# Attention scores in 128x64 tiles, small steps moved between engines, and all weight conversions in the attention stage

## The chip, the cores and the metric

One core of a Trainium2 chip. The metric is the device time of one execution in microseconds (us), the median of several runs. TensorE multiplies (PE; its weight loads are PEld), VectorE (DVE), ScalarE (ACT) and GpSimd (POOL) do the rest, SyncE (SP) issues most of the DMA transfers.

## What is computed

Three stages follow each other. q, k and v are (4, 8, 1152, 64): 4 batches, 8 heads. All arithmetic is fp32 in and out.

```python
def _attn_ref(q, k, v):
    q_pool = q.reshape(B, H, S // 2, 2, D).mean(axis=3)
    scores = scale * np.matmul(q_pool, k.transpose(0, 1, 3, 2))
    scores = scores - np.max(scores, axis=-1, keepdims=True)
    attn = np.exp(scores)
    attn = attn / (np.sum(attn, axis=-1, keepdims=True) + 1e-09)
    return np.matmul(attn, v)
...
# x: the attention's output as 2304 tokens of 512
    logits = x @ w_gate + modality_bias[modality_id]      # 8 experts
    e_idx = np.argmax(logits, axis=1)
    ...
        out[mask] = gate_w[mask, None] * (np.maximum(x[mask] @ w1[e], 0.0) @ w2[e])
...
    h = x @ w_in                                          # 512 -> 2048
    g = np.maximum(h, 0.0) + np.log1p(np.exp(-np.abs(h)))
    return g @ w_out                                      # 2048 -> 512
```

## The kernel before

**Attention** works on 16 pairs of heads, `p`. For each pair the 576 pooled queries come in two halves of 288, the 1152 keys in nine chunks of 128; a round `g` is one chunk of one half, so a pair has 18 rounds and the whole 288. In each round TensorE makes the scores of both heads (`smat`, L163: keys as weights, 288 queries streaming, a high and a low fp16 product each, into PSUM tile `st`), ScalarE takes their exponential (`ex`, L170, tile `P`), GpSimd adds `P` up over three chunks (`add`, L174, tile `acc`; a few sums on VectorE where the table `DVA` says so), and TensorE multiplies `P` with the values (`pv`, L207; fp32, 64 columns of weights for each head, written side by side into two halves of one PSUM tile; it runs for two rounds at a time). Ahead of a pair its row maxima have to be known: `srow` (L109) makes 27 row scores per pair (queries as weights, 384 keys streaming, tile `sr`), VectorE reduces each to a maximum (L121); `mfin` (L123) gathers them, splits them into a high and a low part `nh` and has TensorE write them into the second half of `Q` (L140). Row scores have full width, but for one tile in nine whose two halves are two heads (L120).

`casts` (L72) prepares a pair: pooled queries `qs` (L77), fp16 casts of queries and keys (ScalarE), their low parts (L86 queries, L94 keys, GpSimd). `lstage` (L217) is the routing of half a batch: logits, maximum, one-hot of the expert, rank in the expert, gate; some thirty steps on 96 partitions, each put into a round of its own by `LSTEPS`. After the first rounds the order on every engine in this stage is the one in which the code is written: in each round the next scores, an event or two of that round in turn with row scores, `pv`, the sums.

**Conversions.** `w_in` and `w_out` come as 8-byte floats; a conversion (`convert`, L984) loads 512 KB of them and makes 128x512 fp32 numbers in three integer steps on VectorE (L993 to L995). There are 32. `CH` places 12 of them in attention, with a staging tile `stg` of two buffers; the other 20 run in the experts' stage (`CVN`: behind units 2, 6 and 10 of a block), in the four buffers `mraw` that the experts' weights use too.

**The experts' stage** (`Moe`, L625, and `moe_ffn`, L724) has nine blocks of 256 tokens of one expert, 16 units of 12 products each. `split` (L642) makes a high (ScalarE) and a low fp16 half (VectorE, L653; in each eighth one GpSimd, L650 and L651) of the loaded weights. The splits of the dense weights (L741) run here too. Here TensorE and SyncE keep the written order, and a scheduler sets that of the other engines. **The dense stage** (`Ffn`) follows.

Of the kernel before, what the change touches and what calls it, by code (L numbers as in the profile page):

```python
# [16 lines left out]
def attention(ctx,late,tc,I,C,x_dram,LG,gate,fill,early):  # L17

    nc=tc.nc
# [52 lines left out]
    def casts(p):  # L72
        ka,kb,q=KA[p%NS],KB[p%NS],Q[p%NS]; ve=nc.gpsimd if p==1 else nc.vector
# [22 lines left out]
        if p==0:  # L96
            c0(); cq(0,0)(); ck(0,0)(); cl(0)(); ck(0,1)(); cq(1,0)(); ck(1,0)(); ck(1,1)()
            C['cl1']=cl(1)
            for h in range(2):
# [4 lines left out]
                (7,cq(0,1)),(9,cq(1,1)),(6,ckl(0,0)),(7,ckl(0,1)),(9,ckl(1,0)),(11,ckl(1,1))]  # L104
# [4 lines left out]
    def srow(r):  # L109
        p,w=divmod(r,SRN); t,kh=divmod(w,3)  # L110
        ka,q=KA[p%NS],Q[p%NS]
        if w==0: MX[p]=smp.tile([128,9,3],F32,name="mx")
        sr=srp.tile([128,512],F32,name="sr")
        h,r0=TILES[t]
        k0=kh*KW
        if h<2:
            nc.tensor.matmul(sr[:,:KW],lhsT=q[:,h,0,r0:r0+128],rhs=ka[:,h,k0:k0+KW],start=True,stop=True)  # L117
        else:
            for hh in range(2):
                nc.tensor.matmul(sr[64*hh:64*hh+64,:KW],lhsT=q[:,hh,0,r0:r0+64],rhs=ka[:,hh,k0:k0+KW],start=True,stop=True)  # L120
        nc.vector.tensor_reduce(out=MX[p][:,t,kh:kh+1],in_=sr[:,:KW],axis=AX.X,op=ALU.max,negate=True)  # L121

    def mfin(p,ta=0,tb=9):  # L123
# [30 lines left out]
        return [a,b,c(0),c(1)]+([d(0),d(1)] if ta==0 else [])  # L154
# [19 lines left out]
    def add(g):  # L174

        p,half,c=dec(g)
        for n,G in enumerate(groups(p,half)):
# [7 lines left out]
            else:  # L185
                for h in range(2): nc.gpsimd.tensor_tensor(out=A[:,h],in0=B_[:,h],in1=P[g][:,h],op=ALU.add)  # L186
# [30 lines left out]
    def lstage(b,half,last=False):  # L217

# [38 lines left out]
        def eq():  # L257
            V.scalar_tensor_tensor(out=T('eq',[96,3,8]),in0=z['d'],scalar=0.0,in1=C['iotaE8'].unsqueeze(1).to_broadcast([96,3,8]),op0=ALU.is_equal,op1=ALU.mult)
        def ed():
            nc.scalar.activation(out=T('ed',[96,3,8]),in_=z['d'],func=ACTF.Exp)  # L260
        def ff():
            V.tensor_reduce(out=T('f',[96,3]),in_=z['eq'],axis=AX.X,op=ALU.min)
        def oh():
            if last: V.tensor_tensor(out=OH,in0=C['iotaE8'].unsqueeze(1).to_broadcast([96,3,8]),in1=e3(z['f']),op=ALU.is_equal)
            else:
                for j in range(3): V.tensor_scalar(out=OH[:,j],in0=C['iotaE8'],scalar1=z['f'][:,j:j+1],scalar2=None,op0=ALU.is_equal)
        def ra():
            V.tensor_reduce(out=T('os',[96,8]),in_=OH.rearrange("p t e -> p e t"),axis=AX.X,op=ALU.add)
# [34 lines left out]
        def cm():  # L303
            if last: V.tensor_tensor(out=T('cm',[96,3,17]),in0=RK.unsqueeze(2).to_broadcast([96,3,17]),in1=C['iota128'][:96,1:18].unsqueeze(1).to_broadcast([96,3,17]),op=ALU.is_ge)
# [5 lines left out]
        def rp():  # L310
            V.scalar_tensor_tensor(out=T('rp',[96,3]),in0=RB,scalar=-128.0,in1=RK,op0=ALU.mult,op1=ALU.add)
# [15 lines left out]
    DVA={14:(2,5,8),15:()}  # L327
# [21 lines left out]
    for p in range(2,NPAIR):  # L349
# [3 lines left out]
        for i,f in cs if p<5 else cs[:11]:  # L353
            put(14*p-19+3*i//4 if p<5 else 18*p-37+i,f,0.67 if f.__qualname__.split('.')[-3] in ('cl','ckl') or i==0 else 0)
        if p>=5:
            for n,(i,f) in enumerate(cs[11:]): put(best(18*p-33 if n<2 else 18*p-30,18*p-26),f,0.67)
# [234 lines left out]
CVN=(2,6,10); NBS=9; NB=16; DF=2048; TB=256; NF=9; YW=NF*TB+TB  # L591
# [33 lines left out]
class Moe:  # L625

    def __init__(s,K,ix,ev,P):
        s.K=K; s.nc=K.nc; s.ix=ix; s.ev=ev; s.P=P; s.src=K.x_dram; s.lim=NT*TW; s.raw={}; s.hl={}; s.nload=0; s.nsplit=0; s.xg={}; s.nd=2
# [13 lines left out]
    def split(s):  # L642
# [6 lines left out]
        if n%8==7:  # L649
# [402 lines left out]
```

## Time and profile before

| | us |
|---|---|
| median of three runs | 1153.48 (1151.69 to 1153.79) |
| the profiled execution | 1149.53, its span 1147.7 |
| TensorE busy | 1082.5 (94% of the span) |
| VectorE busy | 865.6 (75%) |
| ScalarE busy | 641.2 (56%) |
| GpSimd busy | 504.9 (44%) |
| attention | 0 to 506 |
| early expert block and routing tables | 506 to 541 |
| nine expert blocks | 541 to 763 |
| dense stage | 763 to 1148 |

The shares are means over stages with different limits; what a change in a stage is worth is read in that stage. A busy row of TensorE is not the time that it streams: a product is pipelined, and its end in the trace is modelled. How fast it goes on is seen from the distance between starts. The stages were told apart by the first and last instruction of their lines.

### The profile page before, as it was taken

What the parts mean: (1) busy time and instruction counts of PE and PEld (TensorE: products, weight loads), DVE (VectorE), ACT (ScalarE), POOL (GpSimd) and SP (SyncE); (2) the same over time, 40 slices, a digit from 0 to 9 for tenths busy, and PEclk for the clock granted to TensorE, in tenths of its full rate; (3) what the DMA queues carried; (4) which work ended last, traced back from release to release, by engine and by line L of the source; (5) the groups of instructions that cost most, each with busy time, mean ns of one, the idle gap of its engine ahead of it and who ended that gap; (6) DMA issues with size and microseconds to landing.
All of it is one profiled execution on the core that took longest, in us unless ns stands there. A gap on an engine that the chain in (4) does not pass through costs nothing. (4 is left out here: it accounts for less than half of the span.)

```text
span 1147.7 us, 20868 instructions
## 1 busy us (share of the span) xinstructions
PE 1082.5 (94%) x7887; PEld 641.0 (56%) x7887; DVE 865.6 (75%) x1583; ACT 641.2 (56%) x1096; POOL 504.9 (44%) x532
## 2 busy tenths in 40 slices
PE   5998999999999999998989898999999999999996
PEld 2444555455555554566877777885444444446662
DVE  5778798768877787969789888739967767676762
ACT  5666656675666655556556556647444444444441
POOL 7888877888688867644423233110000100100101
PEclk9999999999999999999999999999999999999999
DMA  9334427441654041335677787731100000000000
GB/s 250 79 84 111 120 64 197 113 120 38 182 149 113 24 130 53 116 127 193 211 261 253 277 279 271 265 125 46 37 10 28 28 10 19 37 1 11 37 10 31
DMA packets 42940, 129.48 MB, mean 113 GB/s; under 512 B 5841, under 2 KB 12881, under 8 KB 40914
## 3 DMA queue, kind: packets, MB, share of 16 engines
q1 hardware_dynamic: 39794, 118.12, 34.2%
q0 software_dynamic: 3040, 9.96, 2.5%
q8 instruction: 65, 1.06, 0.4%
q14 instruction: 41, 0.34, 0.1%
HBM read 108.13 MB, written 20.45 MB: 112 GB/s over the span
## 5 line engine op out<-in xcount | busy, mean ns | idle before, releaser
L121 DVE TENSOR_REDUCE mx<-sr 128x1 f32<-128x384 f32 x432 | 225.4, 550 | 92.8 <-PE sr L117 73.9
L172 ACT ACTIVATE P<-st 128x576 f32<-128x576 f32 x288 | 186.0, 651 | 154.0 <-PE st L169 142.5
L186 POOL TENSOR_TENSOR acc<-P 128x288 f32<-128x288 f32 x192 | 160.6, 858 | 84.0 <-ACT P L172 80.3
L796 POOL DMA_INDIRECT out_dram<-io,CIDS x18 | 21.1, 1174 | 359.1 <-ACT io L794 312.7
L212 PE MATMUL pv<-P,v 128*64 128x288 f32 x1152 | 174.5, 419 | 0.3 <-ACT P L172 0.3
L168 PE MATMUL st<-Q,KA 128*128 128x288 f16 x576 | 155.4, 291 | 0.0
L169 PE MATMUL st<-Q,KB 128*128 128x288 f16 x576 | 153.6, 288 | 1.8 <-ACT Q L152 1.8
L186 POOL TENSOR_TENSOR acc<-acc,P 128x288 f32<-128x288 f32 x176 | 148.5, 864 | 9.0 <-ACT P L172 7.3
L117 PE MATMUL sr<-KA,Q 128*128 128x384 f16 x384 | 113.6, 335 | 17.2 <-DVE mx L121 8.7
L611 PE MATMUL l<-xf,WIH 128*128 128x256 f16 (+1 forms) x384 | 125.1, 326 | 1.0 <-ACT xf L817 1.0
L612 PE MATMUL l<-xf,WIH 128*128 128x256 f16 (+1 forms) x384 | 125.1, 326 | 0.2 <-DVE xf L818 0.2
L613 PE MATMUL l<-xf,wl 128*128 128x256 f16 (+1 forms) x384 | 125.1, 326 | 0.0
L648 ACT ACTIVATE mhl<-mraw 128x512 f16<-128x512 f32 x160 | 98.1, 625 | 45.3 <-DMA mraw<-in_wm_dram 22.2
L653 DVE SCALAR_TENSOR_TENSOR mhl<-mraw,mhl 128x512 f16<-128x512 f32 x140 | 95.7, 703 | 27.3 <-ACT mhl L648 26.5
L212 PEld LDWEIGHTS pv<-P,v 128*64 128x64 f32 x1152 | 70.4, 136 | 72.9 <-issue 35.6
L787 PE MATMUL o<-WOH,g 128*128 128x512 f16 x288 | 109.1, 379 | 1.2 <-ACT io L794 0.8
L788 PE MATMUL o<-wl,g 128*128 128x512 f16 x288 | 109.1, 379 | 0.0
L789 PE MATMUL o<-WOH,g 128*128 128x512 f16 x288 | 109.1, 379 | 0.0
L168 PEld LDWEIGHTS <-KA 128*128 128x128 f16 x576 | 56.3, 98 | 85.5 <-issue 75.4
L770 ACT ACTIVATE e<-e 128x1024 f32<-128x1024 f32 x36 | 38.0, 1057 | 101.3 <-DVE m L768 101.3
L94 POOL TENSOR_TENSOR KB<-kr,KA 64x576 f16<-64x576 f32 x64 | 83.3, 1305 | 4.3 <-ACT KA L90 2.1
L612 PE MATMUL l<-hT,mhl 128*128 128x256 f16 x288 | 78.5, 272 | 6.4 <-DVE hT L680 6.4
(246 smaller groups left out, 2162.0 us busy)
## 6 DMA issues: line engine op xcount, KB each, us to landing
mraw<-in_wm_dram SPq DMA_DIRECT2D x80, 512.0 KB
kr<-in_k_dram SPq DMA_DIRECT2D x30, 576.0 KB
qr<-in_q_dram SPq DMA_DIRECT2D x16, 576.0 KB
v<-in_v_dram SPq DMA_DIRECT2D x16, 576.0 KB
mraw<-in_w_out_dram SPq DMA_DIRECT2D x16, 512.0 KB
stg<-in_w_in_dram SPq DMA_DIRECT2D x12, 512.0 KB
y_dram<-w SPq DMA_DIRECT2D x20, 256.0 KB
xs_dram<-xs SPq DMA_DIRECT2D x24, 192.0 KB
```

Source lines behind the costliest of these rows:

```text
L117: nc.tensor.matmul(sr[:,:KW],lhsT=q[:,h,0,r0:r0+128],rhs=ka[:,h,k0:k0+KW],start=True,stop=True)
L121: nc.vector.tensor_reduce(out=MX[p][:,t,kh:kh+1],in_=sr[:,:KW],axis=AX.X,op=ALU.max,negate=True)
L168: nc.tensor.matmul(st[:,h,:HQ],lhsT=ka[:,h,ks],rhs=q[:,h,0,qs],start=True,stop=False)
L169: nc.tensor.matmul(st[:,h,:HQ],lhsT=kb[:,h,ks],rhs=q[:,h,1,qs],start=False,stop=True)
L172: nc.scalar.activation(out=P[g],in_=ST.pop(g)[:,:,:HQ],func=ACTF.Exp,scale=1.0/16)
L186: for h in range(2): nc.gpsimd.tensor_tensor(out=A[:,h],in0=B_[:,h],in1=P[g][:,h],op=ALU.add)
L212: nc.tensor.matmul(t[64*h:64*h+64,:HQ],lhsT=V[p][:,c,64*h:64*h+64],rhs=P[g][:,h],start=(c==0),stop=(c==NCH-1))
L611: nc.tensor.matmul(o,lhsT=wh_,rhs=x[0],start=first,stop=False)
L612: nc.tensor.matmul(o,lhsT=wh_,rhs=x[1],start=False,stop=False)
L613: nc.tensor.matmul(o,lhsT=wl_,rhs=x[0],start=False,stop=last)
L787: nc.tensor.matmul(o,lhsT=g[:,0,i,cs],rhs=WOH[:,fc],start=(fc==0),stop=False)
L788: nc.tensor.matmul(o,lhsT=g[:,0,i,cs],rhs=WOL(fc),start=False,stop=False)
```

## The change

- *Tiles.* Scores (`smat`) and row scores (`srow`) are made in two halves of 64 weight columns each, which go to the two halves of the same PSUM tile, as `pv` does already. Twice as many products and loads.
- *Casts.* From pair 2 on, pooled queries and the queries' low parts are made by GpSimd (`ve`), before by VectorE; the keys' low parts stand in later rounds.
- *Sums.* GpSimd adds both heads in one instruction; the second sum of each middle group (`DVA`, c = 4) goes to VectorE in pairs 1 to 13.
- *Maxima.* From pair 2 on, the split into `nh` is made by ScalarE and GpSimd (`a2`), in a round between the gathering and the products.
- *Routing.* In the first three batches (`port`) some steps go to GpSimd, three-fold steps on VectorE become one, the difference to the maximum goes into ScalarE's exponential; `LSTEPS` is stretched by two rounds.
- *Conversions.* `CH` places all 32 in attention; the experts' stage has none.
- *Low halves.* GpSimd makes them in the early block alone (`s.pool`); else VectorE does.

```diff
-        ka,kb,q=KA[p%NS],KB[p%NS],Q[p%NS]; ve=nc.gpsimd if p==1 else nc.vector
+        ka,kb,q=KA[p%NS],KB[p%NS],Q[p%NS]; ve=nc.gpsimd if p else nc.vector
...
-        if h<2:
-            nc.tensor.matmul(sr[:,:KW],lhsT=q[:,h,0,r0:r0+128],rhs=ka[:,h,k0:k0+KW],start=True,stop=True)
-        else:
-            for hh in range(2):
-                nc.tensor.matmul(sr[64*hh:64*hh+64,:KW],lhsT=q[:,hh,0,r0:r0+64],rhs=ka[:,hh,k0:k0+KW],start=True,stop=True)
+        for i in range(2):
+            hh,r=(h,r0+64*i) if h<2 else (i,r0)
+            nc.tensor.matmul(sr[64*i:64*i+64,:KW],lhsT=q[:,hh,0,r:r+64],rhs=ka[:,hh,k0:k0+KW],start=True,stop=True)
...
+        def a2():
+
+            nm,nh=st['nm'],st['nh']; ns=smp.tile([128,9],F32,name="ns")
+            nc.scalar.activation(out=nh[:,:,0],in_=nm,func=ACTF.Copy,scale=1.0/256)
+            nc.scalar.activation(out=ns,in_=nm,func=ACTF.Copy,scale=1.0/256)
+            nc.gpsimd.tensor_tensor(out=nh[:,:,1],in0=ns,in1=nh[:,:,0],op=ALU.subtract)
...
         for h in range(2):
-            nc.tensor.matmul(st[:,h,:HQ],lhsT=ka[:,h,ks],rhs=q[:,h,0,qs],start=True,stop=False)
-            nc.tensor.matmul(st[:,h,:HQ],lhsT=kb[:,h,ks],rhs=q[:,h,1,qs],start=False,stop=True)
+            for i,w in enumerate((ka,kb)):
+                for o in (0,64):
+                    nc.tensor.matmul(st[o:o+64,h,:HQ],lhsT=w[:,h,c*128+o:c*128+o+64],rhs=q[:,h,i,qs],start=(i==0),stop=(i==1))
...
             if c in DVA.get(p,()): nc.vector.tensor_tensor(out=A,in0=B_,in1=P[g],op=ALU.add)
             else:
-                for h in range(2): nc.gpsimd.tensor_tensor(out=A[:,h],in0=B_[:,h],in1=P[g][:,h],op=ALU.add)
+                nc.gpsimd.tensor_tensor(out=A,in0=B_,in1=P[g],op=ALU.add)
...
+        port=b<B-1; G=nc.gpsimd
...
         def eq():
-            V.scalar_tensor_tensor(out=T('eq',[96,3,8]),in0=z['d'],scalar=0.0,in1=C['iotaE8'].unsqueeze(1).to_broadcast([96,3,8]),op0=ALU.is_equal,op1=ALU.mult)
+            if port:
+                V.tensor_tensor(out=T('d',[96,3,8]),in0=lg,in1=e3(z['m']),op=ALU.is_equal)
+                G.tensor_tensor(out=T('eq',[96,3,8]),in0=z['d'],in1=C['iotaE8'].unsqueeze(1).to_broadcast([96,3,8]),op=ALU.mult)
...
-    DVA={14:(2,5,8),15:()}
+    DVA={**{p:(4,) for p in range(1,14)},14:(2,5,8),15:()}
...
-            pend.extend([(g+d,f) for d,f in zip((1,1,1,1,1) if p==1 else (3,3,3,3,2),MF[1:])])
+            pend.extend([(g+d,f) for d,f in zip((1,1,1,1,1) if p<2 else (1,4,4,4,4,4),MF[1:])])
...
-        if n%8==7:
+        if n%8==7 and s.pool:
...
-            if j>=1 and ncv<32 and n in CVN:
-                for z in convert(ncv,P['raw'],"mraw"): z()
-                ncv+=1
...
-CH=((2,1),(3,1),(6,1),(7,1),(10,1),(11,1),(14,6))
+CH=((2,2),(3,3),(4,1),(5,2),(6,3),(7,3),(8,1),(9,2),(10,3),(11,3),(12,1),(13,2),(14,6))
```

TensorE in a round of attention with `pv`, before: a row score, `pv` of two chunks, then the next round's scores (an fp32 product is one row, which loads its own weights).

```order
L117 LDWEIGHTS Q_195
L117 MATMUL sr<-KA_189,Q_195 128x384
L212 MATMUL pv<-P,v 64x288 x4
L168 LDWEIGHTS KA_191
L168 MATMUL st<-Q_197,KA_191 128x288
L169 LDWEIGHTS KB_194
L169 MATMUL st<-Q_197,KB_194 128x288
```

The same place in the changed kernel.

```order
L118 LDWEIGHTS Q_195
L118 MATMUL sr<-KA_189,Q_195 64x384
L118 LDWEIGHTS Q_195
L118 MATMUL sr<-KA_189,Q_195 64x384
L218 MATMUL pv<-P,v 64x288 x4
L175 LDWEIGHTS KA_191
L175 MATMUL st<-Q_197,KA_191 64x288
L175 LDWEIGHTS KA_191
L175 MATMUL st<-Q_197,KA_191 64x288
L175 LDWEIGHTS KB_194
L175 MATMUL st<-Q_197,KB_194 64x288
```

Around `pv`, 128 output rows have become twice 64: the width of the tiles no longer changes there.

GpSimd over some seven rounds of attention, before: the keys' low parts (`KB`) among the sums.

```order
L94 TENSOR_TENSOR KB_194<-kr,KA_191 64x576
L186 TENSOR_TENSOR acc<-P 128x288 x2
L186 TENSOR_TENSOR acc<-acc,P 128x288 x2
L94 TENSOR_TENSOR KB_194<-kr,KA_191 64x576 x2
L186 TENSOR_TENSOR acc<-P 128x288 x2
L186 TENSOR_TENSOR acc<-acc,P 128x288 x2
L94 TENSOR_TENSOR KB_194<-kr,KA_191 64x576
```

GpSimd in the changed kernel, the rounds in which a pair's queries are prepared.

```order
L77 TENSOR_TENSOR qs<-qr 128x576
L192 TENSOR_TENSOR acc<-acc,P 128x576
L192 TENSOR_TENSOR acc<-P 128x576
L86 TENSOR_TENSOR Q_195<-qs,Q_195 64x576
L192 TENSOR_TENSOR acc<-acc,P 128x576
L86 TENSOR_TENSOR Q_195<-qs,Q_195 64x576
L192 TENSOR_TENSOR acc<-acc,P 128x576
L137 TENSOR_TENSOR nh<-ns,nh 128x9
L94 TENSOR_TENSOR KB_192<-kr,KA_189 64x576
```

The queries' steps and the split of the maxima now stand among the sums, which have double width.

VectorE in an expert block, before: a conversion between weight halves (`mhl`) and the hidden layer's low half (`hT`).

```order
L653 SCALAR_TENSOR_TENSOR mhl<-mraw,mhl 128x512
L993 TENSOR_SCALAR w_21_91<-mraw 128x512
L994 SCALAR_TENSOR_TENSOR w_21_91<-mraw,w_21_91 128x512
L680 SCALAR_TENSOR_TENSOR hT<-l,hT 128x2x256
L995 SCALAR_TENSOR_TENSOR w_21_91<-mraw,w_21_91 128x512
L653 SCALAR_TENSOR_TENSOR mhl<-mraw,mhl 128x512 x2
L741 SCALAR_TENSOR_TENSOR wl_9368<-w_21_91,WOH 128x512
L680 SCALAR_TENSOR_TENSOR hT<-l,hT 128x2x256
```

The same dense weight's split (`wl`) in the changed kernel, earlier in the order.

```order
L755 SCALAR_TENSOR_TENSOR wl_10670<-w_20_90,WOH 128x512
L694 SCALAR_TENSOR_TENSOR hT<-l,hT 128x2x256
L667 SCALAR_TENSOR_TENSOR mhl<-mraw,mhl 128x512 x2
L755 SCALAR_TENSOR_TENSOR wl_10725<-w_21_91,WOH 128x512
L694 SCALAR_TENSOR_TENSOR hT<-l,hT 128x2x256
```

The three conversion steps are gone from between them, and 22 of the 32 splits stand within two blocks, one behind nearly every weight half.

## Rows read from the trace of the kernel before

**Rows 1.** Busy time of each engine in stretches (instructions, clock, DMA share, GB/s)
```profile
core 0: us, PE busy (x) PEld busy (x) DVE busy (x) ACT busy (x) POOL busy (x), PEclk, DMA share, GB/s
...
30.00:506.00 476.00, 458.72 (x3676) 238.83 (x3672) 377.77 (x808) 301.01 (x547) 378.57 (x424) 1.00 0.39 107
...
541.00:763.00 222.00, 203.18 (x1820) 174.72 (x1819) 178.00 (x298) 131.80 (x238) 69.81 (x50) 1.00 0.74 251
```

**Rows 2.** Waits, 30 to 506 us: who waited for whom, total, times, longest
```profile
ACT P L172 <- PE st L169: 139.9, 153, 3.6
...
ACT P L172 <- POOL acc L186: 8.7, 18, 1.1
PE sr L117 <- DVE mx L121: 8.0, 10, 2.1
```

**Rows 3.** TensorE's instructions in order from 308.9 us: start, length, what
```profile
308.92 0.33 PE L117 MATMUL sr<-KA,Q 128*128 128x384 f16 x1
309.17 1.19 PE L212 MATMUL pv<-P,v 128*64 128x288 f32 x8
310.30 0.30 PE L168 MATMUL st<-Q,KA 128*128 128x288 f16 x1
310.43 0.29 PE L169 MATMUL st<-Q,KB 128*128 128x288 f16 x1
```

**Rows 4.** The same view from 58.7 us, narrow products behind each other
```profile
58.75 0.52 PE L120 MATMUL sr<-KA,Q 128*64 128x384 f16 x4
59.10 1.14 PE L212 MATMUL pv<-P,v 128*64 128x288 f32 x8
60.17 0.30 PE L168 MATMUL st<-Q,KA 128*128 128x288 f16 x1
```

**Rows 5.** Weight loads in order at 116.4 us: one pair of narrow ones
```profile
116.37 0.11 PEld L120 LDWEIGHTS <-Q 128*64 128x64 f16 x2 [0.24 <-issue]
```

**Rows 6.** Groups by line, 0 to 506 us: count, busy us, mean ns, idle before
```profile
L186 POOL TENSOR_TENSOR acc<-P 128x288 f32<-128x288 f32 x192 | 160.6, 858 | 84.0 <-ACT P L172 80.3 <-POOL KB L94 1.2 <-PE sr L197 0.8
...
L86 DVE TENSOR_TENSOR Q<-qs,Q 64x576 f16<-64x576 f32 x30 | 36.3, 1209 | 2.4 <-ACT Q L81 1.5
...
L995 DVE SCALAR_TENSOR_TENSOR w<-stg,w 128x512 int32<-128x512 int32 x12 | 13.5, 1126 | 0.1
...
L77 DVE TENSOR_TENSOR qs<-qr 128x576 f32<-128x576 f32 x15 | 12.1, 807 | 4.4 <-DMA qr<-in_q_dram 4.4
...
L994 DVE SCALAR_TENSOR_TENSOR w<-stg,w 128x512 int32<-128x512 int32 x12 | 10.3, 861 | 0.1
L266 DVE TENSOR_SCALAR OH<-cc,f 96x8 f16<-96x8 f32 x21 | 10.2, 541 | 0.0
L993 DVE TENSOR_SCALAR w<-stg 128x512 int32<-128x512 int32 x12 | 8.7, 724 | 0.0
...
L132 DVE SCALAR_TENSOR_TENSOR nh<-nm,nh 128x9 f16<-128x9 f32 (+2 forms) x17 | 7.4, 438 | 0.6
...
L184 DVE TENSOR_TENSOR acc<-acc,P 128x576 f32<-128x576 f32 x6 | 4.5, 750 | 0.7 <-POOL acc L186 0.7
...
L77 POOL TENSOR_TENSOR qs<-qr 128x576 f32<-128x576 f32 x1 | 1.4, 1398 | 0.1
```

**Rows 7.** The same view, 541 to 763 us
```profile
L653 DVE SCALAR_TENSOR_TENSOR mhl<-mraw,mhl 128x512 f16<-128x512 f32 x123 | 83.0, 696 | 19.7 <-ACT mhl L648 19.1 <-PE l L613 0.3
...
L650 POOL TENSOR_SCALAR mraw<-mraw 128x512 f32<-128x512 f32 x18 | 27.6, 1534 | 100.5 <-ACT mhl L648 65.9 <-DMA mraw<-in_wm_dram 18.6 <-DVE mhl L653 8.4
...
L995 DVE SCALAR_TENSOR_TENSOR w<-mraw,w 128x512 int32<-128x512 int32 x20 | 15.5, 773 | 0.0
```

**Rows 8.** Waits of TensorE, 541 to 763 us
```profile
PE l L612 <- DVE hT L680: 6.4, 7, 1.0
PE l L613 <- DVE mhl L653: 6.1, 7, 1.3
...
PE l L613 <- POOL mhl L651: 1.8, 3, 0.9
```

More of the change, by code (lines that the diff above doesn't have):

```diff
@@ L257, in eq @@
         def eq():
-            V.scalar_tensor_tensor(out=T('eq',[96,3,8]),in0=z['d'],scalar=0.0,in1=C['iotaE8'].unsqueeze(1).to_broadcast([96,3,8]),op0=ALU.is_equal,op1=ALU.mult)
+            if port:
+                V.tensor_tensor(out=T('d',[96,3,8]),in0=lg,in1=e3(z['m']),op=ALU.is_equal)
+                G.tensor_tensor(out=T('eq',[96,3,8]),in0=z['d'],in1=C['iotaE8'].unsqueeze(1).to_broadcast([96,3,8]),op=ALU.mult)
+            else: V.scalar_tensor_tensor(out=T('eq',[96,3,8]),in0=z['d'],scalar=0.0,in1=C['iotaE8'].unsqueeze(1).to_broadcast([96,3,8]),op0=ALU.is_equal,op1=ALU.mult)
         def ed():
-            nc.scalar.activation(out=T('ed',[96,3,8]),in_=z['d'],func=ACTF.Exp)
+            if port:
+                T('ed',[96,3,8])
+                for j in range(3): nc.scalar.activation(out=z['ed'][:,j],in_=lg[:,j],func=ACTF.Exp,scale=-1.0,bias=z['m'][:,j:j+1])
+            else: nc.scalar.activation(out=T('ed',[96,3,8]),in_=z['d'],func=ACTF.Exp)
         def ff():
@@ L263, in oh @@
         def oh():
-            if last: V.tensor_tensor(out=OH,in0=C['iotaE8'].unsqueeze(1).to_broadcast([96,3,8]),in1=e3(z['f']),op=ALU.is_equal)
+            if last or port: V.tensor_tensor(out=OH,in0=C['iotaE8'].unsqueeze(1).to_broadcast([96,3,8]),in1=e3(z['f']),op=ALU.is_equal)
             else:
@@ L272, in gb @@
         def gb():
-            V.tensor_scalar(out=g,in0=g,scalar1=1e-9,scalar2=1.0/SX,op0=ALU.add,op1=ALU.mult)
+            (G if port else V).tensor_scalar(out=g,in0=g,scalar1=1e-9,scalar2=1.0/SX,op0=ALU.add,op1=ALU.mult)
         def gc():
@@ L276, in gd @@
         def gd():
-            if last: V.tensor_tensor(out=z['r'].rearrange("p (t a) h -> p t (a h)",t=3),in0=z['r'].rearrange("p (t a) h -> p t (a h)",t=3),in1=e3(g),op=ALU.mult)
+            if last or port: (G if port else V).tensor_tensor(out=z['r'].rearrange("p (t a) h -> p t (a h)",t=3),in0=z['r'].rearrange("p (t a) h -> p t (a h)",t=3),in1=e3(g),op=ALU.mult)
             else:
@@ L303, in cm @@
         def cm():
-            if last: V.tensor_tensor(out=T('cm',[96,3,17]),in0=RK.unsqueeze(2).to_broadcast([96,3,17]),in1=C['iota128'][:96,1:18].unsqueeze(1).to_broadcast([96,3,17]),op=ALU.is_ge)
+            if last or port: V.tensor_tensor(out=T('cm',[96,3,17]),in0=RK.unsqueeze(2).to_broadcast([96,3,17]),in1=C['iota128'][:96,1:18].unsqueeze(1).to_broadcast([96,3,17]),op=ALU.is_ge)
             else:
@@ L310, in rp @@
         def rp():
-            V.scalar_tensor_tensor(out=T('rp',[96,3]),in0=RB,scalar=-128.0,in1=RK,op0=ALU.mult,op1=ALU.add)
+            if port:
+                G.tensor_scalar(out=T('rp',[96,3]),in0=RB,scalar1=-128.0,scalar2=None,op0=ALU.mult)
+                G.tensor_tensor(out=z['rp'],in0=z['rp'],in1=RK,op=ALU.add)
+            else: V.scalar_tensor_tensor(out=T('rp',[96,3]),in0=RB,scalar=-128.0,in1=RK,op0=ALU.mult,op1=ALU.add)
         def oi(j):
@@ L352, in attention @@
         cs=casts(p)
[L353 to L356, printed above, removed]
+        for i,f in cs: put(14*p-19+3*i//4 if p<5 else 18*p-37+i,f)
     last=0
@@ L722, in step, with moe_ffn @@
             if s.todo: s.K.unit(s.todo.pop(0))
-def moe_ffn(ctx,mst,tc,I,C,Y,YE,wsp,W32,out,convert,ncv,K,P,bl):
+def moe_ffn(ctx,mst,tc,I,C,Y,YE,wsp,W32,out,K,P,bl):
     nc=tc.nc
@@ L1009, in tile_kernel @@
         with ExitStack() as c2:
-            moe_ffn(c2,mst,tc,I,C,Y,YE,wsp,W32,out,convert,sum(n for _,n in CH),K,P,bl)
+            moe_ffn(c2,mst,tc,I,C,Y,YE,wsp,W32,out,K,P,bl)
 def lay(inp):
```

27 lines of the change are left out of this document (14 added, 13 removed).

## Prediction

> **What bounds the kernel now.** I read the busy time by stage first. In the attention stretch (30 to 506 us) TensorE is busy for 458.7 of 476 us, VectorE for 377.8, GpSimd for 378.6, ScalarE for 301.0; in the mixture-of-experts stretch (541 to 763 us) TensorE for 203.2 of 222 us [rows 1]. The dense stretch behind is not touched. Then the waits of the attention stretch, to see whether TensorE is the one that others wait for: ScalarE's exponentials sat idle for 139.9 us until the scores came, while TensorE waited for VectorE's row maxima for 8.0 us, and the exponentials for GpSimd's sums for 8.7 [rows 2]. So attention is paced by TensorE, with two engines at four fifths close behind.
>
> Last I read TensorE's own list for what it does with its time, since a busy row does not say that the array streams. The clock is granted in full there [rows 1], which is the 2.4 GHz level, so 384 columns are 0.16 us, 288 are 0.12, and an fp32 product of 288 columns, which streams each column twice, 0.24. A product in half the array's columns shares that time with its partner in the other half: eight such pv rows come in four pairs, 0.96 us. But in the list the one full-width row score at 308.92 is followed by pv only 0.25 later, and pv at 309.17 by the next full-width score only 1.13 later; the second full-width score then comes 0.13 behind [rows 3]. Of these 1.38 us 1.12 are streaming. Where pv follows narrow row scores instead, two pairs and four pairs start 0.35 and then 1.07 us apart from what follows, against 0.32 and 0.96 [rows 4]: no step of 0.09 between L120 and L212, and 0.06 less inside pv. So **a change of tile width costs about 0.09 us going in, about 0.10 coming out**, and the first pair behind it 0.05 more if it is pv (0.03 for fp16 scores), the first wide one 0.01. A visit to pv and back costs 0.25.
>
> **The change part by part.** *Scores in half-width tiles.* Each full-width product becomes two of 64 columns, over the same 288 or 384 columns of the moving side. Their streaming time stays if the two run side by side, as the narrow row scores L120 do today: four of them, two pairs, 0.35 us [rows 4]. What goes are width changes. Counted along TensorE's list between the first and the last score, the kernel before has 486 of them, that is 243 visits, 176 of these from full width to 64 columns; the changed one has 202: 53 visits to the 32-column sums, 33 to full-width transposes and rank products, 15 to half-height ones. The step in and out of 142 visits, at 0.19 to 0.20, is 28 us. The first-pair extras fall from about 140 x 0.05 (pv first) + 36 x 0.03 + 226 x 0.01 = 10 us to 20 x 0.05 + 66 x 0.03 + 33 x 0.01 = 3. Together **-35 us** of TensorE's time, all in the stage that it paces. Not shown anywhere: narrow fp16 behind narrow fp32, which is what scores behind pv now are. The nearest rows bound it: 0 (fp32 behind fp16 in one width, 58.75 to 59.10) and 0.10 (the step out of pv); I take 0, since there both type and width are as here but for their order.
>
> The weight loads double in number. A pair of them, 64 columns each, stands in the list with 0.11 us for both, side by side [rows 5], and a pair of scores streams for 0.12: it fits with 0.01 to spare, and nothing is added. The Trainium skill speaks against this part: "TensorEngine Tiling (Array Packing)", Feature Incompatibilities, says that column tiling excludes the fast weight load. By that page the loads would be dearer; the rows have them dearer too, and still covered, so the rule becomes the slower rival below and not a term.
>
> *VectorE's and GpSimd's shares.* VectorE gives up 28 casts at 1.209, 14 pooled queries at 0.807, 28 small steps of the maxima at about 0.4 and 72 routing steps of at most 0.541 (I take 0.36 for one, and 0.2 for each of the 18 that replace them) [rows 6]: -34 - 11 - 11 - 22 = -78 us. It takes 26 sums at 0.750 and 20 conversions of three steps, 0.724 + 0.861 + 1.126 = 2.71 [rows 6]: +19.5 + 54.2 = +74. So VectorE stays at about 374 us. GpSimd merges its sums: 368 at 0.86 become 158 of twice the width. Their price lies between the one 128x576 sum of GpSimd in the trace, 1.398, and two halves, 1.72 [rows 6]; I take 1.40, as that is the same shape and types: 221 for 316 us. It takes 42 casts and pooled queries at up to 1.398 (59) and 50 small steps at about 0.3, an estimate between nothing and its shortest sum of 0.86 (15). So -21 us, or +30 with the upper price: 358 us, at most 410. Against an attention stretch of about 441 us these are 85% and 81%, from 79% and 80% now. The cover thus stays, but thinner, and three new hand-offs stand in rings that TensorE waits for: ScalarE's query casts behind GpSimd's pooled query; the bias products (L140) behind ScalarE and GpSimd; VectorE's routing steps behind GpSimd. What is queued behind a late one is ScalarE's next exponential, or all of VectorE's maxima. The waits shown now, 8.0 and 8.7 us [rows 2], came about at four fifths; I let them grow by a third, **+6 us** (ends -10, if the lighter routing chain frees VectorE there, and +25).
>
> The 20 loads of 512 KB that go along stand in SyncE's queue in attention, where the DMA engines are at 0.39 of their time [rows 1]; they cost nothing there, and if they ran late they would hold only VectorE's conversions, which nothing in attention reads.
>
> *The experts' stretch.* It loses 20 conversions from VectorE and from the four weight buffers, and 18 low halves go from GpSimd (1.534 and a second step) to VectorE (0.696) [rows 7]. TensorE's waits there are 6.4 us for the low half of the hidden layer, 6.1 for VectorE's weight halves, 1.8 for GpSimd's [rows 8], 14.3 together, and most of these stand right behind a conversion or a slow GpSimd half. But with the conversions gone the dense weights' splits (22 of the 32) move forward into two blocks, between the experts' weight halves, so these two blocks stay as tight as they are. I take three quarters of the waits: **-11 us** (ends -6 and -16).
>
> The sum: -35 + 6 - 11 = -40. The profiled execution took 1149.5 us, 4.0 less than the median of 1153.5; the sum is made against the former, 1109.5, and lifted by those 4.0: **1113 us**.
>
> **The rivals.** *GpSimd and VectorE block each other* (1134). The last conversion step takes 1.126 us in attention and 0.773 among the experts, where GpSimd is idle for most of the time [rows 6, 7], so the two engines do slow each other. If they excluded each other wholly, GpSimd's 358 us and VectorE's two-operand steps, 32 x 2.71 + 26 x 0.75 = 106, would stand in series: 464 us and the odd stall, some 468, instead of 447. Gain 8 + 11 = 19. Against it: the maxima overlap GpSimd freely, and the same sum before, 379 + 12 x 2.71 + 45 = 456, was below the 476 and could not show. "SBUF — State Buffer", Who interferes with whom, of the Trainium skill, says just this: one shared pair of ports, an exclusive lock; by that rule this rival's 1134 holds.
>
> *It doesn't do what it says* (1128): the step out of pv belongs to the type, not to the width, and stays at the about 150 places where scores follow pv: 150 x 0.10 = 15 us of the 35 are not won. The row for it is missing; against it speaks that fp32 behind fp16 in one width costs nothing [rows 4].
>
> *The half-width loads are not covered* (1223, slower than before): if the two loads of a pair ran one behind the other, 0.22 us, a pair would take 0.22 and not 0.12: 288 x 4 pairs x 0.10 = 115 us more, less 46 won: +69. It decides as soon as two loads take longer than 0.12 together. Against it: the pair in rows 5 took 0.11.
>
> *The waits go too* (1093): the routing chain and the maxima no longer meet on VectorE, and the 17 us of waits shrink to a few instead of growing.
>
> **How the numbers follow.** Forecast 1113: 0.66. Blocked engines 0.13, step stays 0.06, waits go 0.07: all faster, 0.92. Loads uncovered 0.05. The last 0.03 is for no change, several of the middle cases at once. The forecast's own ends are 35 + 10 + 16 = 61 and 35 - 25 + 6 = 16 below 1153.5, 1092 and 1137; both at once is unlikely, so the range is **1095 to 1136**, which takes in the two middle rivals. A measurement of this kernel tells about 0.2% (2.3 us) from no change. Faster by more than that 0.92, within it 0.03, slower 0.05.
>
> **What would show it.** Right: the attention stretch ends near 475 us after the start instead of 506; scores 0.12 us per pair; no gap between pv and the scores; exponentials still waiting for scores; the experts' stretch about 211 us. Wrong: pairs of scores 0.2 us apart (loads), 0.10 between pv and the next score (type), TensorE idle in attention with GpSimd over 95% busy, or ScalarE's casts waiting for GpSimd for more than 20 us.

## The result and the profile after

The changed kernel takes **1142.1 us** (median; 1138.4 to 1147.5) against 1152.6 for the kernel before in the same session: ratio **0.9915**, 95% interval 0.9899 to 0.9931. So it is faster, by about 10 us and not by the 40 that were predicted, and it lies outside the range. The profiled execution took 1146.6 us, 4.5 more than the median; its span is 1144.8.

Busy time by stretch in the changed kernel, with the attention stretch first and the experts' behind it (columns as in [rows 1]):

```profile
core 0: us, PE busy (x) PEld busy (x) DVE busy (x) ACT busy (x) POOL busy (x), PEclk, DMA share, GB/s
30.00:518.00 488.00, 443.04 (x5161) 304.24 (x5159) 413.78 (x736) 305.44 (x588) 381.95 (x308) 0.97 0.45 125
...
555.00:760.00 205.00, 198.88 (x1818) 175.88 (x1817) 149.26 (x258) 130.11 (x238) 19.64 (x14) 1.00 0.67 219
```

Set beside [rows 1], the experts' stretch is 17 us shorter, more than forecast. But attention, which should have become 31 us shorter, is **longer**: its last pv product ends at 520.0 us after the start, before at 506.2. TensorE was busy for 458.7 of 476 us and is now busy for 443 of 488; VectorE went from 378 to 414; and the clock's mean fell to 0.97.

Who waited for whom in the attention stretch of the changed kernel (us in total, times, longest):

```profile
ACT P L178 <- PE st L175: 129.2, 149, 3.3
DVE mx L119 <- PE sr L118: 66.8, 100, 2.3
...
POOL acc L192 <- DVE acc L190: 37.2, 16, 4.8
POOL acc L192 <- ACT P L178: 23.5, 15, 5.0
PE sr L118 <- DVE mx L119: 19.5, 25, 2.3
...
PE sr L203 <- DVE mx L119: 8.8, 7, 2.7
...
ACT P L178 <- POOL acc L192: 5.8, 5, 2.0
...
PE sr L145 <- DVE nh L131: 5.6, 2, 3.7
```

TensorE's row scores waited 8.0 us for VectorE's maxima before [rows 2]; the row scores and the row sums (L203) now wait 28.3, and GpSimd's sums wait 37.2 us for VectorE's. Another 5.6 us are two waits of the bias products (L145) of the first two head pairs.

Yet the width change itself went as forecast. TensorE's list, start and length, at 258.5 us:

```profile
258.50 0.29 PE L175 MATMUL st<-Q,KB 128*64 128x288 f16 x2
258.63 0.33 PE L118 MATMUL sr<-KA,Q 128*64 128x384 f16 x2
258.79 1.14 PE L218 MATMUL pv<-P,v 128*64 128x288 f32 x8
259.76 0.29 PE L175 MATMUL st<-Q,KA 128*64 128x288 f16 x2
259.88 0.29 PE L175 MATMUL st<-Q,KB 128*64 128x288 f16 x2
```

Row score to pv 0.16, four pv pairs 0.97, pairs of scores 0.12: nothing but streaming, where [rows 3] had 0.25 and 1.13. I added up, for the list from 30 us to the last pv, what lies between one start and the next beyond streaming time at 2.4 GHz and 0.1 us per width change (I call the rest TensorE's **stalls**). Streaming is 391 us in both kernels. The width changes fall from 486 to about 205, 46.4 to 19.9 us. The stalls rise from 33.0 to **73.5**. That is the whole story of the stretch: -26.5 + 40.5 = +14 us. (In both kernels the three add up to some 6 us less than the stretch, so a figure of the stalls is good to about 5 us.)

**Where a stall comes from.** The longest VectorE step of the stretch, with GpSimd's instructions beside it and TensorE behind:

```profile
154.19 0.55 DVE L119 TENSOR_REDUCE mx<-sr 128x1 f32<-128x384 f32 x1
...
154.54 1.40 POOL L77 TENSOR_TENSOR qs<-qr 128x576 f32<-128x576 f32 x1
154.66 4.56 DVE L1006 SCALAR_TENSOR_TENSOR w<-stg,w 128x512 int32<-128x512 int32 x1
...
155.91 1.40 POOL L192 TENSOR_TENSOR acc<-acc,P 128x576 f32<-128x576 f32 x1
...
157.27 1.39 POOL L192 TENSOR_TENSOR acc<-P 128x576 f32<-128x576 f32 x1
159.14 1.47 DVE L119 TENSOR_REDUCE mx<-sr 128x1 f32<-128x384 f32 x3
159.83 0.69 PE L203 MATMUL sr<-acc,one 128*32 128x288 f32 x8 [2.67 <-DVE mx L119]
```

The third conversion step takes 0.68 us where no GpSimd instruction overlaps it; here it takes 4.56. It starts 0.12 us behind a GpSimd instruction, stands through that one and through the two that follow it without a gap, and ends 0.55 us after the last. The longest step is as long, 4.56 us, in e3 and e10 below. Three row maxima are queued behind it, the maxima's three buffers are full, and TensorE stands for 2.67 us. Then this (stretches of the changed kernel; the granted clock is the third number from the end):

```profile
157.20:159.80 2.60, 0.00 (x0) 0.00 (x1) 2.60 (x3) 1.62 (x3) 1.46 (x2) 1.00 0.28 105
161.10:164.50 3.40, 3.40 (x24) 2.00 (x20) 0.65 (x2) 1.44 (x3) 2.63 (x2) 0.50 0.00 0
```

Behind the stall the clock is at 0.50, the 1.2 GHz level, and pairs of scores follow 0.24 us apart instead of 0.12. This happens eight times in attention, once for twice as long. Each time it begins near the end of a stand of TensorE of 1.9 to 3.7 us, between 1.5 us before that end and 1.4 us after it. Two of the eight are behind the bias products' waits (L145), the others behind waits for the maxima. But not every such stand has it. At 142.6 us the clock stayed at 1.00 behind one of 2.18 us, as long as two of the eight:

```profile
142.58 0.35 PE L118 MATMUL sr<-KA,Q 128*64 128x384 f16 x2 [2.18 <-DVE mx L119]
```

The kernel before has a single wait over 1.6 us there, 2.1 us [rows 2], and its clock did not fall in the profiled execution. That one was favourable: its mean granted clock is 0.998, that of 38 later executions of the same kernel 0.991 to 0.997; the changed kernel's 15 executions have 0.984 to 0.989.

VectorE's groups in the attention stretch of the changed kernel (count, busy us, mean ns):

```profile
L119 DVE TENSOR_REDUCE mx<-sr 128x1 f32<-128x384 f32 x409 | 213.8, 549 | 69.2 <-PE sr L118 66.8
L1006 DVE SCALAR_TENSOR_TENSOR w<-stg,w 128x512 int32<-128x512 int32 x32 | 42.3, 1321 | 0.1
L1005 DVE SCALAR_TENSOR_TENSOR w<-stg,w 128x512 int32<-128x512 int32 x32 | 39.9, 1248 | 0.1
L1004 DVE TENSOR_SCALAR w<-stg 128x512 int32<-128x512 int32 x32 | 29.8, 932 | 0.0
L190 DVE TENSOR_TENSOR acc<-P 128x576 f32<-128x576 f32 x26 | 24.6, 945 | 0.0
L332 DVE TENSOR_SCALAR OHID<-cc,rp 96x128 f16<-96x128 f32 x18 | 14.9, 855 | 0.0
```

A conversion costs 3.50 us here, 2.71 in the kernel before [rows 6], and 0.42 + 0.68 + 0.68 = 1.78 where no GpSimd instruction overlaps (means of six, two and one steps). The maxima, which read PSUM, are 0.549 with and without GpSimd.

### The profile page after: what moved, and what is told of

It reads as the page before. It is cut to its first block, busy times and chain, and to the rows that moved or that the text cites. A ratio compares the mean times of both kernels' runs of the same rounds, so it can differ in the third digit from the quotient of the medians.

```text
span 1144.8 us, 23612 instructions
## 1 busy us (share of the span) xinstructions
PE 1064.5 (93%) x9423; PEld 711.0 (62%) x9423; DVE 874.7 (76%) x1479; ACT 643.2 (56%) x1136; POOL 457.4 (40%) x378
## 5 line engine op out<-in xcount | busy, mean ns | idle before, releaser
L118 PE MATMUL sr<-KA,Q 128*64 128x384 f16 x864 | 138.1, 345 | 32.4 <-DVE mx L119 20.1
L175 PE MATMUL st<-Q,KB 128*64 128x288 f16 x1152 | 161.5, 293 | 2.1 <-ACT Q L157 2.1
L175 PE MATMUL st<-Q,KA 128*64 128x288 f16 x1152 | 162.2, 294 | 0.0
L667 DVE SCALAR_TENSOR_TENSOR mhl<-mraw,mhl 128x512 f16<-128x512 f32 x158 | 111.4, 716 | 49.3 <-ACT mhl L662 47.6
L192 POOL TENSOR_TENSOR acc<-acc,P 128x576 f32<-128x576 f32 x88 | 128.9, 1465 | 42.1 <-DVE acc L190 37.2
L192 POOL TENSOR_TENSOR acc<-P 128x576 f32<-128x576 f32 x70 | 102.6, 1467 | 24.4 <-ACT P L178 23.9
L218 PEld LDWEIGHTS pv<-P,v 128*64 128x64 f32 x1152 | 86.9, 141 | 35.1 <-issue 6.2
L118 PEld LDWEIGHTS <-Q 128*64 128x64 f16 x864 | 57.9, 113 | 59.2 <-issue 43.9
L94 POOL TENSOR_TENSOR KB<-kr,KA 64x576 f16<-64x576 f32 x64 | 89.2, 1400 | 4.3 <-ACT KA L90 2.4
L175 PEld LDWEIGHTS <-KB 128*64 128x64 f16 x1152 | 73.8, 113 | 26.7 <-issue 3.1
```

The source lines that it names most:

```text
L118: nc.tensor.matmul(sr[64*i:64*i+64,:KW],lhsT=q[:,hh,0,r:r+64],rhs=ka[:,hh,k0:k0+KW],start=True,stop=True)
L175: nc.tensor.matmul(st[o:o+64,h,:HQ],lhsT=w[:,h,c*128+o:c*128+o+64],rhs=q[:,h,i,qs],start=(i==0),stop=(i==1))
L192: nc.gpsimd.tensor_tensor(out=A,in0=B_,in1=P[g],op=ALU.add)
L218: nc.tensor.matmul(t[64*h:64*h+64,:HQ],lhsT=V[p][:,c,64*h:64*h+64],rhs=P[g][:,h],start=(c==0),stop=(c==NCH-1))
L667: s.nc.vector.scalar_tensor_tensor(out=t[:,1],in0=r,scalar=SW,in1=t[:,0],op0=ALU.mult,op1=ALU.subtract)
```

## The experiments

Two theories stood against each other. **Hold**: VectorE steps with their operands in SBUF stand still while GpSimd works, the maxima behind them are late, TensorE stalls, its clock falls. **Load**: VectorE simply has more in its queue between two maxima. A third, **hand-offs**, lays the stalls to the new ways through ScalarE and GpSimd. (In the expectations Hold is theory L, Load is theory Q and hand-offs are theory C.) All runs are in one table; "attention" is the end of the last pv product, "behind" is from there to the first product with w_out (experts and the start of the dense layer), busy times are from 30 us to the end of attention. Ratios are against the kernel before in the same session, where it took 1152.6 to 1155.3 us; small differences are better read from them than from the medians. All columns behind the ratio are of one profiled execution, which lies up to 7 us from its kernel's median (e8):

| kernel | median us | ratio (95%) | attention | behind | VectorE, GpSimd busy | stalls |
|---|---|---|---|---|---|---|
| before | 1152.6 | 1 | 506.2 | 277.7 | 378, 379 | 33.0 |
| changed | 1142.1 | 0.9915 (0.9899-0.9931) | 520.0 | 260.7 | 416, 382 | 73.5 |
| e1 half width alone | 1138.9 | 0.9855 (0.9802-0.9908) | 492.3 | 285.4 | 383, 377 | 47.8 |
| e2 all but half width | 1161.3 | 1.0059 (1.0036-1.0082) | 531.4 | 264.5 | 409, 381 | 58.5 |
| e3 20 conversions back | 1129.0 | 0.9785 (0.9741-0.9829) | 486.5 | 276.1 | 357, 366 | 41.3 |
| e4 steps without hold | 1105.1 | 0.9580 (0.9536-0.9623) | 482.4 | 256.8 | 366, 362 | 37.5 |
| e5 the same, equal load | 1127.5 | 0.9775 (0.9726-0.9825) | 501.4 | 261.2 | 411, 361 | 55.8 |
| e6 sums in halves | 1138.2 | 0.9849 (0.9808-0.9889) | 512.7 | 259.5 | 411, 411 | 65.6 |
| e7 32 through PSUM | 1125.7 | 0.9751 (0.9714-0.9788) | 502.3 | 257.2 | 384, 359 | 57.6 |
| e8 12 through PSUM | 1129.1 | 0.9763 (0.9732-0.9794) | 491.7 | 278.7 | 348, 361 | 45.2 |
| e9 20 through PSUM | 1124.7 | 0.9741 (0.9723-0.9760) | 489.4 | 265.5 | 359, 361 | 44.5 |
| e10 e3, sums on GpSimd | 1136.8 | 0.9841 (0.9814-0.9869) | 494.9 | 276.3 | 332, 399 | 48.6 |
| e11 e8, later bias products | 1126.6 | 0.9768 (0.9720-0.9816) | 486.2 | 273.3 | 346, 361 | 40.6 |
| e12 e9 + e11, more sums on VectorE | 1120.6 | 0.9704 (0.9674-0.9734) | 484.3 | 266.7 | 371, 327 | 39.2 |

### The parts of the change, one by one

**e1**, the kernel before with nothing but the new `srow` and `smat`:

> The kernel before with nothing but the scores in half-width tiles. Theory L (lock): a VectorE step that reads and writes SBUF stands still while GpSimd runs an instruction; the maxima queued behind it come late, TensorE stalls for 1 to 3 us and its clock falls to 0.5 behind the stall. Here GpSimd (379 us) and VectorE's steps of that kind (12 conversions at 1.78, 30 query casts at 0.75, pooled queries 11, sums 4.5, small steps some 15) want about 453 us one behind the other, against 441 of TensorE: attention ends at 485 to 495, the experts' stretch stays at 222, about 1137. The prediction's own sum: -35 and a few us of waits, attention ends near 478, 1118 to 1122. Theory W (the width change is not what was paid): no gain, 1150.

Measured 1138.9, attention to 492.3: theory hold's numbers. The width changes went as in the changed kernel (to 208), but 14 us of the stretch were won and not 35: stalls rose from 33 to 47.8 with nothing added to any other engine; some 5 us of that is the clock, which stood at 0.50 for 10 us. A faster TensorE runs into VectorE and GpSimd, now at 83 and 82% of a shorter stretch.

**e2**, the reverse, the changed kernel with `srow` and `smat` of before:

> The changed kernel with the scores back in full-width tiles, all else as changed: what the other parts do alone. Theory L: TensorE's list is as long as before, 476 us in attention, GpSimd and VectorE's SBUF steps want 475 to 480 one behind the other, and the stalls come on top: attention ends at 515 to 530 (506 before), the experts' stretch is 17 us shorter as in the changed kernel: 1150 to 1158. The prediction's sum: +6 - 11, about 1148, attention ends at 512.

Slower than before, 1161.3, attention to 531, both just beyond the bound given for hold and far from the sum's 1148. Without the half-width tiles the rest of the change is a loss of 0.6%.

**e3**, the changed kernel with the conversions shared out as before:

```diff
-CH=((2,2),(3,3),(4,1),(5,2),(6,3),(7,3),(8,1),(9,2),(10,3),(11,3),(12,1),(13,2),(14,6))
+CH=((2,1),(3,1),(6,1),(7,1),(10,1),(11,1),(14,6))
...
+            if j>=1 and ncv<32 and n in CVN:
+                for z in convert(ncv,P['raw'],"mraw"): z()
+                ncv+=1
```

> The changed kernel with 20 of the 32 conversions back among the experts, as before. Theory L: 60 of VectorE's 96 held steps leave attention (70 us of its 112 us for conversions), GpSimd and the SBUF steps want 442 us, TensorE's stalls fall from 73 to about 40 and few clock drops stay: attention ends at 485 to 495 instead of 520, the experts' stretch goes back up by some 15: about 1130. Theory C (the stalls come from the new hand-offs: bias products through ScalarE and GpSimd, query casts on GpSimd): stalls stay at 60 to 70, attention ends at 510 or later, 1150.

1129.0, attention to 486.5, stalls 41.3. Hand-offs are out as the main cause: they are all still there. Twenty conversions cost attention 33.5 us, 1.7 each, and give the stretch behind 15.4, 0.77 each. That would be a net loss of 18 us, as between the two profiled executions; by the medians it is 13. Both differences hold some of the clock: it stood at 0.50 in attention for 31 us in the changed kernel and 7 in e3, and behind attention for none and 7. Against e1 the rest of the change, the moved small steps and the low halves, gained 10.

### Hold or load

**e4** and **e5** keep every VectorE instruction of a conversion in its place, but as a reduction, which GpSimd does not stretch, of the free length (e4) and of the held length (e5). They leave out the conversion itself:

```diff
-                def b(): nc.vector.tensor_scalar(out=dst,in0=z['s'][:,:,1],scalar1=3,...)
+                def b(): nc.vector.tensor_reduce(out=W32[i],in_=z['s'].bitcast(F32)[:,:,1:2],axis=AX.X,op=ALU.max)
...
# e5: in_=z['s'].bitcast(F32)[:,:,1:2].to_broadcast([128,512,2])
```

> The changed kernel with each of the three steps of a conversion replaced by a reduction over one element, which copies the high words: so the weights of the dense layer are not the converted ones. The number of VectorE instructions, their places, the loads and the elements stay. Reductions are not stretched by GpSimd in the trace (0.531 us free, 0.540 beside it). Theory L: the 96 steps take the same time beside GpSimd as without it (some 0.6 us each, 58 us instead of 112), TensorE's stalls fall from 73 us to 35 to 45, the clock falls once or twice instead of 8 times, attention ends at 485 to 495: 1110 to 1118. Theory Q (the places: a step in the row of the maxima delays them by its own length, lock or no lock): the stalls stay over 60 us, 1138 to 1144.

> As the run with reductions in place of the conversion steps (the weights of the dense layer are again not the converted ones), but each reduction goes over two elements, 1024 in all, so that a step takes about 1.15 us: 96 steps, 110 us of VectorE, as much as the 112 us that the held steps of the changed kernel take, only evenly and at no time waiting for GpSimd. If VectorE's mere load makes TensorE stall (theory Q), nothing is won: 1138 to 1144, stalls 65 to 75 us. If it is the long waits, of which one step in ten has over 1.8 us and the longest 4.6 (theory L), TensorE's stalls fall to about 45 and the clock falls at most three times: 1110 to 1122.

The three steps in e4 (attention stretch, as above):

```profile
L1006 DVE TENSOR_REDUCE w<-stg 128x512 f32<-128x512 f32 x32 | 21.8, 681 | 0.1
L1005 DVE TENSOR_REDUCE w<-stg 128x512 f32<-128x512 f32 x32 | 21.7, 677 | 0.1
L1004 DVE TENSOR_REDUCE w<-stg 128x512 f32<-128x512 f32 x32 | 21.6, 675 | 1.1 <-DMA stg<-in_w_out_dram 1.1
```

0.68 us each, at most 0.72, though nearly all overlap GpSimd; attention ends at 482.4 and 37 us are won, more than hold forecast. The same steps in e5:

```profile
L1006 DVE TENSOR_REDUCE w<-stg 128x512 f32<-128x1024 f32 x32 | 38.7, 1209 | 0.1
L1005 DVE TENSOR_REDUCE w<-stg 128x512 f32<-128x1024 f32 x32 | 38.7, 1209 | 0.1
L1004 DVE TENSOR_REDUCE w<-stg 128x512 f32<-128x1024 f32 x32 | 38.6, 1206 | 0.0
```

They take 1.21 us each, 116 us, as evenly, a little more than the 112 of the held steps: 1127.5, between the two expectations, which both fail. So the 37 us come apart in about 15 that equal VectorE time gives back once it is even (changed to e5), and 22 for the length itself (e5 to e4). Both are the hold's: it makes the steps long, and it makes them uneven. Yet the 22 also say that load is half right: VectorE's time costs even where it is not held. And the 15 are not VectorE's evenness alone, for GpSimd is freed too: its sums go from 1.47 to 1.42 us in e4 and e5, its busy time from 382 to 362 and 361. The runs do not separate these two.

**e6**, GpSimd's sums in two instructions of 288 columns again:

```diff
-                nc.gpsimd.tensor_tensor(out=A,in0=B_,in1=P[g],op=ALU.add)
+                for h in range(2): nc.gpsimd.tensor_tensor(out=A[:,h],in0=B_[:,h],in1=P[g][:,h],op=ALU.add)
```

> The changed kernel with GpSimd's 158 sums again in two instructions of 288 columns each. Theory G (the length of one GpSimd instruction sets how long a VectorE step is held): the holds go from up to 1.4 to up to 0.8 us, the three steps of a conversion from 3.5 to about 3.0 us, stalls fall by 10 to 15 us: 1130 to 1135. Theory F (GpSimd's share sets it: a step gets in only when GpSimd has nothing to do): GpSimd goes from 382 to about 420 us, holds grow, 1145 to 1160.

Neither. A conversion did not become shorter: its first step did, from 0.93 to 0.67, but the others went to 1.41 and 1.53, 3.6 us in all. GpSimd was busier, 411 us, which may be why. Still the time was 4 us below the changed kernel's. The clock fell four times in attention instead of eight, which can account for that; I did not separate it further.

**e10** puts 26 sums from VectorE back on GpSimd in e3 (`DVA={14:(2,5,8),15:()}`):

> The kernel with 20 conversions back (12 in attention through SBUF, 1129), and the 26 sums that had gone to VectorE back on GpSimd. If VectorE's own load makes TensorE stall, 26 sums of 0.95 to 1.3 us less, 25 to 34 us, give 3 to 8 us: 1121 to 1126. If GpSimd's share does it (366 us would become some 404 of 457, and every step that is held waits longer), 1133 to 1142.

1136.8, 8 us slower (6 by the ratios, whose intervals just overlap), though VectorE has 25 us less to do. The time is as forecast for GpSimd's share, the way is not: the twelve conversions were not held longer (3.46 us, 3.60 in e3). GpSimd itself was late at 399 of 465 us: the exponentials waited 14.3 us for its sums (7.7 in e3), TensorE's row sums 5.8 (3.7), and the clock stood at 0.50 for 17 us of the stretch (7 in e3).

### Versions

**e7** makes the converted numbers again, in steps that have at most one operand in SBUF and write to PSUM or read from it. The three steps of a half follow each other in one place; before, each step of a conversion had a place of its own:

```diff
+                def half(k):
+                    def f():
+                        w=slice(256*k,256*k+256); hi=z['s'][:,w,1]; lo=z['s'][:,w,0]
+                        t=srp_[0].tile([128,512],F32,name="sr").bitcast(I32)[:,:256]
+                        nc.vector.tensor_scalar(out=t,in0=hi,...)
+                        nc.vector.scalar_tensor_tensor(out=t,in0=hi,...,in1=t,...)
+                        nc.vector.scalar_tensor_tensor(out=dst[:,w],in0=lo,...,in1=t,...)
+                    return f
```

> The changed kernel with all 32 conversions in attention, computed as before, but each in two halves of 256 columns, and with the intermediate words in a PSUM tile of the maxima's ring instead of in SBUF, so that no step has both operands, or operand and result in the fast form, in SBUF. Theory L: no step waits for GpSimd, a conversion takes about 2.1 us (six steps of about 0.35) instead of 3.5, TensorE's stalls fall from 73 to 40 to 45 us: attention ends near 485, 1106 to 1116. Rival R: one of the three buffers of the ring is held for 1.1 us at a time, TensorE waits there: stalls of 55 to 65, 1122 to 1132. Rival N: the operand in PSUM changes nothing: steps stretched as now, 1140 or more.

The steps in e7:

```profile
L1009 DVE SCALAR_TENSOR_TENSOR sr<-stg,sr 128x256 int32<-128x256 int32 x64 | 27.5, 430 | 2.2
L1010 DVE SCALAR_TENSOR_TENSOR w<-stg,sr 128x256 int32<-128x256 int32 x64 | 26.9, 421 | 2.2
L1008 DVE TENSOR_SCALAR sr<-stg 128x256 int32<-128x256 int32 x64 | 26.7, 417 | 0.4 <-DMA stg<-in_w_out_dram 0.4
```

The hold is gone (none over 0.45 us), so rival N falls; but six steps of 0.42 are 2.5 us and not 2.1, and the time is rival R's. TensorE now waits for the buffer:

```profile
PE sr L118 <- DVE w L1010: 7.8, 9, 1.3
...
PEld L118 <- DVE w L1010: 4.6, 3, 1.6
```

How much of the time the buffer costs, and how much the steps' new places, was not separated.

**e8** and **e9** do 12 and 20 conversions that way and leave the rest to the experts' stretch; **e11** is e8 with the bias products of the first two head pairs one or two chunks later (`(3,3,3) if p==0 else (2,2,2,2,2) if p==1`); **e12** is e9 with that and with `DVA={**{p:(4,7) ...` for `(4,)`.

> Half-width scores and the moved casts, sums and small steps, with 20 of the 32 conversions back among the experts, and the 12 left in attention by way of a PSUM tile, in halves of 256 columns. Measured so far: 20 back, the 12 through SBUF, 1129; all 32 through PSUM, 1125.7. If what a conversion costs in attention is VectorE's time and the buffer held, about 0.8 us through PSUM and 1.7 through SBUF, the 12 give back some 8 to 10 us of VectorE's 47 for them: attention ends at 480 to 483, 1121 to 1126. If the hold of the ring's buffer is dearer than the wait for GpSimd when conversions are few, 1129 or more.

> The same with 20 conversions in attention by way of PSUM and 12 among the experts. One conversion costs about 0.8 us in attention by this way and 0.77 in the experts' stretch (15.4 us for 20), so the place makes no difference any more: 1121 to 1127, within 0.3% of the run with 12. If the cost in attention grows with their number (the maxima's ring is then held more often when VectorE is late already), it is 2 to 4 us slower than that.

> The run with 12 conversions through PSUM, with the bias products of the first two head pairs issued one or two chunks later. In the changed kernel TensorE stands 2.0 and 3.9 us there, behind VectorE's two steps for them, 1.7 and 2.5 us each because GpSimd holds them (0.18 us free), and the clock is at 0.5 behind both stalls. Later, the products find their operand ready: 5 to 6 us of stalls and one or two clock drops of at most 1.7 us go: 4 to 8 us less than without, 1115 to 1120. If the wait only moves to who needs the product (the scores of the second pair), no change.

> The run with 20 conversions through PSUM (1124.7), with the later bias products, and with 26 more sums (one more per chunk group of nine) from GpSimd to VectorE: the opposite of the run that put sums back on GpSimd, which cost 8 us. VectorE takes 26 x 0.95 = 25 us more, GpSimd 38 us less (about 320 of 455). If GpSimd's share is what costs, through the holds, TensorE's stalls fall by 5 to 8 us: 1115 to 1120. If VectorE's own load costs as much by now (it goes to some 395 of 455), no change or slower: 1124 to 1132.

e8 came out at 1129.1, where its second branch begins, but its interval does not tell it from e3: with 12 conversions these runs show no difference between the ways. e9 came in the expected time. e11 missed: 4.6 us fewer stalls in its profile, but 1126.6 against 1129.1 is within the intervals. e12, the opposite of e10, ends just above its 1115 to 1120 and is the fastest kernel that makes all conversions, 1120.6 us, **2.96% below before** (2.66 to 3.26); its interval still overlaps e9's.

## Why the prediction was wrong

**Right.** TensorE's saving: 486 changes to 202 forecast, 486 to 205 measured, 26.5 us for 28; no step between pv and scores, which takes the rival "it doesn't do what it says" out; loads 0.11 under pairs of 0.12, which takes out "not covered". The 20 moved loads cost nothing. The experts' stretch: -17 in the profile for -11, just beyond its ends of -6 and -16. In the changed kernel TensorE's waits there fell from 6.4 and 6.1 us [rows 8] to this:

```profile
PE l L626 <- DVE hT L694: 1.4, 2, 1.0
...
PE l L627 <- DVE mhl L667: 1.2, 4, 0.3
```

GpSimd's 1.8 is gone too. So 11.7 of the 14.3 us of these waits went, about the three quarters that were forecast; the other 5 of the 17 were not in those rows. In e3 the two waits are 6.1 and 6.7 us again: it was the conversions. By e3 their departure is worth up to 15.4 of the 17. What the low halves on VectorE are worth is not shown: e1, whose code there is that of before, took 285.4 us behind attention against 277.7.

**Wrong: the step in which VectorE stays at about 374 us and the waits grow by a third, +6 us.** TensorE's stalls grew by 40.5 us, although the first-pair extras, forecast to fall by 7, are counted in them. Three things are in it.

1. *The conversions' price.* I took 2.71 us from [rows 6] as if it belonged to the step. It was a mean over twelve steps partly held; with 32 of them, GpSimd's sums 1.47 us long and its added casts 1.37 to 1.46, it became 3.50. The 20 added cost some 79 us of VectorE and not 54, and the sums on VectorE 0.95 and not 0.75. Of VectorE's 414 against 374 some 30 us are these two. GpSimd came out at 382 us instead of 358, its sums at 1.47 instead of 1.40. The price of the free step, 1.78, and the held one should have stood as two ends of a range that depends on GpSimd's share.
2. *The waits.* VectorE at 85% and GpSimd at 78% were no cover for a TensorE that needs a maximum every 1.2 us (409 in 488) through three buffers. e1 shows it with no other edit: half of what TensorE gained came back as stalls.
3. *The clock*, which the prediction has nowhere. Products that started in the low stretches lost about 12 us in the profiled execution, more than a quarter of the growth. The profile of before gave no row for it, with its clock at 1.00 throughout attention [rows 1].

**The rival that was right in kind.** "GpSimd and VectorE block each other" had 0.13 and 1134. Its place and mechanism hold: a step with its operands in SBUF was held up to 4.56 us, reductions and steps with one operand in PSUM were not (0.68 and 0.42 with and without GpSimd). "SBUF — State Buffer", Who interferes with whom, of the Trainium skill, which the rival cited, states an exclusive lock on one shared pair of ports; the traces agree, with these numbers. The rival's price was wrong: I put the two engines' work in series, 464 us and an odd stall, and argued that the maxima overlap freely. They do, but they stand in VectorE's queue behind the held step; the stretch took 490 us, 478 without the clock's 12. And that the sum of 456 stayed below the 476 of before was no evidence against it: with TensorE's share cut to 441, the same sum would have bound.

## What to carry to other kernels

Cost a VectorE step by what GpSimd does beside it, with the free and the held duration as two ends, and look for a form that is not held (a reduction, one operand in PSUM) before moving work there. When the pacing engine is made faster, take each partner's share of the new, shorter stretch, and ask how many buffers stand between a late partner and the pacing engine; here, at 83%, half of the gain came back as waits (e1), and with the load added all of it. Try the parts of a change apart: here one part won 15 us (e1), the moved small steps and low halves 10 (e3 against e1), and the conversions gave 13 back (changed against e3).

## What the runs showed of the hardware

- In these traces a waiting VectorE step was not served between GpSimd instructions that followed without a gap: it stood through three (4.56 us). At 239.7 us, where a gap of 0.08 us came after the second, the step got in there and ended after 2.82 us, and the third GpSimd instruction took 1.73 instead of 1.39:

```profile
239.35 1.27 POOL L94 TENSOR_TENSOR KB<-kr,KA 64x576 f16<-64x576 f32 x1
...
239.72 2.82 DVE L1006 SCALAR_TENSOR_TENSOR w<-stg,w 128x512 int32<-128x512 int32 x1
...
240.59 1.39 POOL L192 TENSOR_TENSOR acc<-P 128x576 f32<-128x576 f32 x1
...
242.06 1.73 POOL L192 TENSOR_TENSOR acc<-acc,P 128x576 f32<-128x576 f32 x1
```

- Around the end of stands of 1.9 to 3.7 us TensorE's granted clock was 0.50 for 3.4 us, once for 6.8, eight times in the changed kernel's attention; behind one stand of 2.18 us there, and behind the one of 2.1 us in the kernel before, it was not. A stall can thus cost more than itself.
- A VectorE step of 256 columns with its result or one operand in PSUM took 0.42 to 0.43 us, beside GpSimd or not. One of 512 columns from SBUF to SBUF took 0.42 (one operand) or 0.68 (two) where no GpSimd instruction overlapped it.
